# Attention top-32 selection: seven blocks of 82 to 84 columns, masks of three tiles on ScalarE, and a check that reads a PSUM bank

## The chip, the cores and the metric

The kernel runs on one core of one Trainium2 chip. A core has a matrix engine (TensorE, in the profile PE, its weight loads PEld), a vector engine (VectorE, DVE), an activation engine (ScalarE, ACT), a general engine (GpSimd, POOL), SyncE (SP), which issues most transfers here, and 16 DMA engines. They run side by side, each through its own list of instructions in order, and wait for each other by semaphores. Work memory is SBUF; TensorE writes to PSUM, eight banks that VectorE and ScalarE can read and write too. The metric is the time of one execution on the device in microseconds (us), the median of three.

## The reference

Three layers run one after the other on float32 data. Attention has 4 batches, 8 heads, 576 positions of width 64; the two layers of experts that follow are not touched by the change.

```python
B, H, S, D = q.shape                                   # 4, 8, 576, 64
scores = scale * np.matmul(q, k.transpose(0, 1, 3, 2))
kth = np.partition(scores, -32, axis=-1)[..., -32:-31]  # the 32nd largest of a row
scores = np.where(scores >= kth, scores, -1e9)
scores = scores - np.max(scores, axis=-1, keepdims=True)
attn = np.exp(scores)
attn = attn / (np.sum(attn, axis=-1, keepdims=True) + 1e-09)
return np.matmul(attn, v)
...
x = _moe_ref(x, ...)      # router over 8 experts, one expert per token, 512 -> 1024 -> 512
return _moe2_ref(x, ...)  # 512 -> 2048 -> 512 for every token
```

So each of 18,432 rows of 576 scores needs its exact 32nd largest value; everything below it is dropped.

## The kernel before

**Tiles.** Two heads make a pair, and a pair's 1152 rows make nine tiles of 128 rows (j = 0 to 7 hold four tiles of one head each, j = 8 the last 64 rows of both heads). 16 pairs make 144 tiles.

**One tile.** TensorE computes its scores into PSUM (L165), ScalarE copies them to SBUF (`ss`, L176). VectorE takes the eight largest of each of eight blocks of 72 columns (L186, one MAX8 a block), which gives 64 candidates (`cand`). From these it takes the largest 24 in five instructions: the largest eight (L195), these struck out (L196), the next eight (L197), struck out (L198), the next eight (L199); the 24th goes into `w`. ScalarE compares the whole row with the 24th candidate (L252: `sg`, with the count in `c1`) and takes the exponential (L257). GpSimd multiplies row and signs (L263, `z`), so that all that lies above the 24th turns negative, and VectorE takes the largest eight of z (L208): with the count, these and the 24th hold the 32nd value, which L209 picks out (`kth`). The mask row >= kth is made by VectorE (L218) for most tiles, and for the tiles of a pair named in `SIGN`, j = 0 and j = 4, by ScalarE as a sign (L243), for which VectorE first makes a negative threshold of one column (L214, `nk`). GpSimd multiplies mask and exponential (L269, `pm`), TensorE transposes the product in five pieces (L289), ScalarE copies these to SBUF (L294, L296) and drops the sign's negative values on the way, and TensorE multiplies them with the values (L310).

**What sets the order.** The loop in `tiles` runs over iterations. In iteration i each step works on another tile, by the lags in `ORDER` (L351): scores and their copy for tile i+1, block maxima for i, selection, signs and z for i-1, the exponential for i-2, the 32nd value for i-3, the mask for i-4, transposes for i-6, output for i-7. In VectorE's list of an iteration (`dve_step`) the mask comes first, then block maxima and selection steps take turns, then the steps of the 32nd value. In ScalarE's list the sign mask comes before the copies of the transposes, and these before the copy of the next scores, the sign and the exponential. Small work of other kinds is put into the gaps: transposing the next pair's queries and keys (L145, L151, in the iterations of j = 1, 3, 5), dividing the outputs (L342 to L346), turning a finished pair for the router (L573 to L584), and for each finished batch the router's products and steps (L593 to L703) and its scatter (L728).

**The check.** For each batch `check` looks whether any 32nd or 24th value is not positive, and notes it in `bad`; then a general path runs at the end in place of the fast one. Its steps stand one an iteration behind the router's steps of the batch. `own` hands out columns of one PSUM bank that VectorE uses for small operands.

**After attention** come the expert products on TensorE (from about 530 us), whose first weights and rows are loaded while attention ends.

Of the kernel before, what the change touches and what calls it, by code (L numbers as in the profile page):

```python
# [12 lines left out]
F32 = mybir.dt.float32  # L13
# [4 lines left out]
OP = mybir.AluOpType  # L18
AX = mybir.AxisListType
PSUM = bass.MemoryType.PSUM  # L20

P = 128
B, H, S, D = 4, 8, 576, 64
NPAIR = H // 2
KB = 8
BW = S // KB
CK = 116
NCK = 5
# [6 lines left out]
def thirds(a):  # L35
    return a.rearrange("p (a b) -> p a b", a=3)


class Job:


    def __init__(self, n, b, hp, j, st):
        self.n, self.b, self.hp, self.j, self.st = n, b, hp, j, st
        self.pre = None
# [5 lines left out]
class Attention:  # L50
    def __init__(self, ctx, tc, q, k, v, sb, ident):
        self.tc, self.nc = tc, tc.nc
        self.q, self.k, self.v = q, k, v
        self.ident = ident
        nc = self.nc
        self.wk = ctx.enter_context(tc.tile_pool(name="attn", bufs=2))
        self.ps = ctx.enter_context(tc.tile_pool(name="attn_ps", bufs=1, space=PSUM))
        one = ctx.enter_context(tc.tile_pool(name="attn_one", bufs=1))

        self.new_pt1()  # L60
        self.new_po()
        self.new_s()

        self.bank = self.ps.tile([P, 512], F32, name="own")
        self.taken = 0
        self.vt = []
        for i in range(3):
            t = one.tile([CK, NCK, 2, D + 1], F32, name=f"vt{i}")
            nc.gpsimd.memset(t, 0.0)
            nc.gpsimd.memset(t[:, :, :, D:D + 1], 1.0)  # L70
            self.vt.append(t)
        self.qm = []
        for i in range(2):
            t = one.tile([P, P], F32, name=f"qm{i}")
            nc.gpsimd.memset(t, 0.0)
            self.qm.append(t)
        self.pb = []
        for i in range(3):
            t = one.tile([P, NCK * CK], F32, name=f"pm{i}")
            nc.vector.memset(t[:, S:], 0.0)  # L80
            self.pb.append(t)
        vsel = one.tile([P, 9, 2], F32, name="vsel")
        nc.gpsimd.iota(vsel, pattern=[[2, 9], [1, 2]], base=S - 2 * TOP, channel_multiplier=0,
                       allow_small_or_imprecise_dtypes=True)
        nc.vector.memset(vsel[:, 0, 1:2], -float(S + 1))
        self.vsel = self.own(18).rearrange("p (a b) -> p a b", b=2)
        nc.vector.tensor_copy(self.vsel, vsel)
        self.rden = self.own(6)
        self.fac = self.own(2)
        nc.vector.memset(self.fac[:, 0:1], -0.125)  # L90
        nc.vector.memset(self.fac[:, 1:2], TINY)
        self.bad = sb.tile([P, 1], F32, name="bad")
        nc.vector.memset(self.bad, 0.0)
        self.per = NPAIR * 9
# [11 lines left out]

    def check(self, st):

        wk, n, v = self.wk, self.per, self.nc.vector
        kth, sm = st  # L110
        d = wk.tile([P, n], F32, name="ckd", bufs=1)
        m = wk.tile([P, 1], F32, name="ckm", bufs=1)
        return [NEXT, lambda: v.tensor_tensor(d, kth, sm[:, :, 1], op=OP.min),
                NEXT, lambda: v.tensor_reduce(m, d, axis=AX.X, op=OP.min),
                NEXT, lambda: v.scalar_tensor_tensor(self.bad, m, 0.0, self.bad, op0=OP.is_le, op1=OP.max)]

    def load(self, b, hp):
        nc = self.nc
# [59 lines left out]
    def dve_step(self, A, Bt, C, M, E, slot):  # L178


        nc, wk = self.nc, self.wk
        blocks, sel, fin = [], [], []
        if A is not None:
            A.cand = wk.tile([P, KB, 8], F32, name="cand", bufs=3)
            for i in range(KB):
                blocks.append(lambda i=i: nc.vector.max(A.cand[:, i], A.ss[:, i * BW:(i + 1) * BW]))  # L186
        if Bt is not None:
            cf = Bt.cand.rearrange("p a b -> p (a b)")
            m = Bt.n % self.per
            if m % 2 == 0:  # L190
                self.w = wk.tile([P, 2, 32], F32, name="w", bufs=3)
            ww = self.w
            w = Bt.w = ww[:, m % 2]
            Bt.sm = Bt.bt[1][:, m]
            sel = [lambda: nc.vector.max(w[:, 0:8], cf),  # L195
                   lambda: nc.vector.match_replace(cf, w[:, 0:8], cf, -1e30),  # L196
                   lambda: nc.vector.max(w[:, 8:16], cf),  # L197
                   lambda: nc.vector.match_replace(cf, w[:, 8:16], cf, -1e30),  # L198
                   lambda: nc.vector.max(w[:, 16:24], cf)]  # L199
            if m % 2:  # L200
                sel.append(lambda: nc.vector.tensor_tensor(
                    Bt.bt[1][:, m - 1:m + 1], ww[:, :, 0:24:23], self.fac[:, None, :].to_broadcast([P, 2, 2]),
                    op=OP.mult))
        if C is not None:
            i = C.n % self.per
            C.kth = C.bt[0][:, i:i + 1]
            scr = wk.tile([P, 9, 2], F32, name="scr", bufs=4)
            fin = [lambda: nc.vector.max(C.w[:, 24:32], C.z),  # L208
                   lambda: nc.vector.scalar_tensor_tensor(scr, self.vsel, C.c1,  # L209
                                                          C.w[:, 23:32, None].to_broadcast([P, 9, 2]), op0=OP.is_equal,  # L210
                                                          op1=OP.mult, accum_out=C.kth)]
            if C.j in self.SIGN:
                C.nk = wk.tile([P, 1], F32, name="nk", bufs=2)
                fin.append(lambda: nc.vector.tensor_scalar(C.nk, C.kth, -TINY, None, op0=OP.mult))  # L214
        fin_at = 5
        chain = sel[:5]
        if M is not None and M.j not in self.SIGN:
            nc.vector.tensor_scalar(self.new_mask(M), thirds(M.ss), M.kth, None, op0=OP.is_ge)  # L218
        for i in range(KB):
            if blocks:  # L220
                blocks[i]()
            if chain:
                chain.pop(0)()
            elif sel[5:]:
                sel.pop()()
                sel = sel[:5]
            if i >= fin_at - 1 and fin:
                fin.pop(0)()
            if i == 2 and E is not None and self.dve_evac(E):
                self.st_evac_v(E)  # L230
            slot(i)
        for f in fin:
            f()

    SIGN = (0, 4)

    def new_mask(self, T):
        T.mg = self.wk.tile([P, 3, S // 3 + 4], F32, name="mg")[:, :, :S // 3]
# [2 lines left out]
    def st_sign2(self, T):  # L241
        if T.j in self.SIGN:
            self.nc.scalar.activation(self.new_mask(T), thirds(T.ss), AF.Sign, bias=T.nk)  # L243
# [191 lines left out]
NEXT = None  # L435
# [1172 lines left out]
```

## Time and profile before

| | |
|---|---|
| median of 3 runs (lowest, highest) | 1232.92 us (1229.69, 1234.66) |
| profiled execution, its own time | 1234.27 us |
| span of its instructions | 1232.6 us |
| TensorE busy, of the span | 1175.5 us |
| VectorE busy | 895.8 us |
| GpSimd busy | 721.5 us |
| ScalarE busy | 688.5 us |

The profile is one execution; its own time is 1.67 us longer than the span of its instructions, and it lies 1.35 us above the median of the runs. The busy times are means over stages with different limits, so they have to be read stage by stage: the attention stage fills about the first 510 us. An instruction's duration in the profile overlaps with the next one on the same engine; how much an engine's list gets longer by it is read from the starts of two that follow each other, or from its share of a chain of waits that runs on this engine alone.

### The profile page before, as it was taken

To read this page: it belongs to the slowest core of one execution; us is meant where nothing else is said; L and a number is where in the kernel's file an instruction comes from. 1 tells how busy PE (TensorE), PEld (TensorE's weight loads), DVE (VectorE), ACT (ScalarE), POOL (GpSimd) and SP (SyncE) were. 2 spreads that over 40 slices of the span, in tenths; PEclk is the share of its full clock that TensorE was granted. 3 is DMA by queue.
4 is the path that set the end of the run, shared out by engine and by line. 5 is a ranking of instruction groups with operands and counts; after the bars stand their busy time and mean duration, and the time that the engine had idled before them with its cause. 6 is when DMAs were issued, how large, how long until landed. Compare 5 with 4: busy or idle time off the path is not lost.

```text
span 1232.6 us, 23943 instructions
## 1 busy us (share of the span) xinstructions
PE 1175.5 (95%) x7729; PEld 1028.1 (83%) x7729; DVE 895.8 (73%) x3769; ACT 688.5 (56%) x1479; POOL 721.5 (59%) x684
## 2 busy tenths in 40 slices
PE   7999999999998999998999899989999999999996
PEld 4777778777876787898999799989899898898995
DVE  5999999999999999885635376767657564454450
ACT  5899989988898988744434255523222322122120
POOL 4898888998899888852424344445335342333331
PEclk9999999999999999888999999989999999999998
DMA  5343221311131113158866678452232121222211
GB/s 132 105 109 103 57 55 52 93 52 49 53 90 36 33 32 121 39 139 194 221 148 202 169 216 222 145 138 86 69 103 86 52 69 54 84 69 69 78 43 55
DMA packets 121539, 120.86 MB, mean 98 GB/s; under 512 B 73380, under 2 KB 91300, under 8 KB 121404
## 3 DMA queue, kind: packets, MB, share of 16 engines
q1 hardware_dynamic: 118492, 109.78, 32.6%
q0 software_dynamic: 2912, 9.46, 2.1%
q8 instruction: 63, 1.03, 0.4%
q14 instruction: 72, 0.59, 0.2%
HBM read 84.25 MB, written 33.92 MB: 96 GB/s over the span
## 4 chain that ended last, share of the span: by engine, by line
PE 46%; DVE 40%; DMA 7%; issue 2%; ACT 2%; POOL 2%; POOLq 0%; SPq 0%; DVEq 0%; ACTq 0%
DVE cand L186 12%; PE mm L990 9%; PE mm L991 9%; PE mm L989 9%; DVE w L208 7%; DVE mg L218 6%; PE mm L1207 5%; PE mm L1206 5%; PE mm L1205 5%; DMA yt<-y 5%; DVE cand L198 2%; DVE cand L196 2%; DMA raw<-in_moe_w 2%; DVE scr L209 2%; DVE w L195 1%
## 5 line engine op out<-in xcount | busy, mean ns | idle before, releaser
L989 PE MATMUL mm<-xT,wt 128*128 128x256 f32 (+7 forms) x852 | 249.4, 293 | 12.0 <-ACT y L1125 6.1
L990 PE MATMUL mm<-xT,wt 128*128 128x256 f32 (+7 forms) x852 | 250.1, 294 | 4.4 <-DVE xT L984 4.3
L186 DVE MAX8 cand<-ss 128x8 f32<-128x72 f32 x1152 | 244.9, 222 | 10.1 <-ACT ss L176 10.1
L991 PE MATMUL mm<-xT,wt 128*128 128x256 f32 (+7 forms) x852 | 249.5, 293 | 0.0
L263 POOL TENSOR_TENSOR z<-ss,sg 128x576 f32<-128x576 f32 x143 | 201.7, 1411 | 64.3 <-ACT sg L252 45.0
L310 PEld LDWEIGHTS po<-vt,pT 116*128 116x128 f32 x1440 | 175.1, 192 | 36.6 <-issue 23.9
L269 POOL TENSOR_TENSOR pm<-e,mg 128x576 f32<-128x576 f32 x141 | 198.8, 1410 | 0.5
L310 PE MATMUL po<-vt,pT 116*128 116x130 f32 x1440 | 197.3, 283 | 1.8 <-ACT pc L342 1.7
L1190 POOL TENSOR_TENSOR hT<-xr,hT 128x256 fp32r<-128x256 f32 x144 | 106.3, 743 | 153.2 <-ACT hT L1189 146.2
L989 PEld LDWEIGHTS mm<-xT,wt 128*128 128x128 f32 x852 | 164.3, 193 | 13.8 <-ACT y L1125 6.6
L1189 ACT ACTIVATE hT<-xr 128x256 fp32r<-128x256 f32 x144 | 59.0, 416 | 200.8 <-DVE xr L1186 194.3
L165 PE MATMUL s<-qk 64*128 64x288 f32 x512 | 166.3, 447 | 3.8 <-ACT ss L176 3.2
L990 PEld LDWEIGHTS mm<-xT,wt 128*128 128x128 f32 x852 | 164.5, 193 | 5.5 <-DVE xT L984 4.5
L991 PEld LDWEIGHTS mm<-xT,wt 128*128 128x128 f32 x852 | 164.9, 194 | 0.0
L924 POOL TENSOR_TENSOR wt<-raw,wt 128x1024 fp32r<-128x1024 f32 x29 | 76.7, 2648 | 98.0 <-ACT wt L923 97.8
L1185 DVE TENSOR_SCALAR xr<-mm,alpha 128x256 f32<-128x256 f32 x144 | 69.3, 481 | 85.1 <-PE mm L991 84.3
L165 PEld LDWEIGHTS s<-qk 64*128 64x128 f32 x512 | 89.6, 194 | 43.2 <-issue 13.4
L252 ACT ACTIVATE sg<-ss,w 128x576 f32<-128x576 f32 x144 | 111.5, 775 | 19.4 <-DVE w L199 17.6
L289 PE MATMUL pt<-ident,pm 128*116 128x128 f32 x720 | 107.3, 278 | 12.5 <-DVE tT L584 7.4
L176 ACT ACTIVATE ss<-s 128x576 f32<-128x576 f32 x144 | 94.0, 653 | 36.6 <-PE s L165 36.3
L257 ACT ACTIVATE e<-ss,sm 128x576 f32<-128x576 f32 x144 | 110.7, 769 | 0.0
L208 DVE MAX8 w<-z 128x8 f32<-128x576 f32 x144 | 106.9, 743 | 0.8 <-POOL z L263 0.8
(248 smaller groups left out, 2490.7 us busy)
## 6 DMA issues: line engine op xcount, KB each, us to landing
raw<-in_moe_w SPq DMA_DIRECT2D x60, 512.0 KB
xr<-yt SPq DMA_DIRECT2D x18, 512.0 KB
xs<-zeros SPq DMA_DIRECT2D x8, 1028.0 KB
raw<-in_moe_w_in SPq DMA_DIRECT2D x16, 512.0 KB
raw<-in_moe_w_out SPq DMA_DIRECT2D x16, 512.0 KB
yt<-zeros SPq DMA_DIRECT2D x8, 704.0 KB
rows<-in_q SPq DMA_DIRECT2D x32, 144.0 KB
rows<-in_k SPq DMA_DIRECT2D x32, 144.0 KB
```

The costliest lines, as they stand in the source:

```text
L165: nc.tensor.matmul(s[:, g, :HALF], qs, t["qk"][hs, S + g * HALF:S + (g + 1) * HALF], start=True, stop=True)
L186: blocks.append(lambda i=i: nc.vector.max(A.cand[:, i], A.ss[:, i * BW:(i + 1) * BW]))
L208: fin = [lambda: nc.vector.max(C.w[:, 24:32], C.z), lambda: nc.vector.scalar_tensor_tensor(scr, self.vsel, C.c1, C.w[:, 23:32, None].to_br ...
L252: nc.scalar.activation(T.sg, T.ss, AF.Sign, bias=T.w[:, 23:24], scale=-ABOVE, accum_out=T.c1)
L257: nc.scalar.activation(T.e, T.ss, AF.Exp, bias=T.sm[:, 0:1], scale=0.125)
L263: eng.tensor_tensor(T.z, T.ss, T.sg, op=OP.mult)
L269: eng.tensor_tensor(thirds(T.pm[:, :S]), thirds(T.e), T.mg, op=OP.mult)
L289: nc.tensor.transpose(o, T.pm[:, c * CK:(c + 1) * CK], self.ident)
L310: nc.tensor.matmul(po[:, i:i + 2, :], T.pT[:, c], rhs, start=(c == 0), stop=(c == NCK - 1))
L989: nc.tensor.matmul(ps, wh, xh, start=first, stop=False)
L990: nc.tensor.matmul(ps, wh, xl, start=False, stop=False)
L991: nc.tensor.matmul(ps, wl, xh, start=False, stop=last)
```

## The change

Three edits. `KB` goes from 8 to 7: seven blocks, six of 82 columns and the last of 84, so 56 candidates in place of 64; the loop in `dve_step` still has eight places, the eighth without a block. `SIGN` goes from tiles 0 and 4 to tiles 0, 3 and 6 of each pair. `check` makes three reductions (of `kth`, of every second column of `sm`, of the two results) into three columns of VectorE's PSUM bank, and its last step reads the result there; before it took the minimum of the two SBUF tensors, reduced it to SBUF and read it there. One step more, so one iteration more.

```diff
-KB = 8
+KB = 7
 BW = S // KB
...
+        self.least = self.own(3)
...
-        d = wk.tile([P, n], F32, name="ckd", bufs=1)
-        m = wk.tile([P, 1], F32, name="ckm", bufs=1)
-        return [NEXT, lambda: v.tensor_tensor(d, kth, sm[:, :, 1], op=OP.min),
-                NEXT, lambda: v.tensor_reduce(m, d, axis=AX.X, op=OP.min),
-                NEXT, lambda: v.scalar_tensor_tensor(self.bad, m, 0.0, self.bad, op0=OP.is_le, op1=OP.max)]
+        return [NEXT, lambda: v.tensor_reduce(m[:, 0:1], kth, axis=AX.X, op=OP.min),
+                NEXT, lambda: v.tensor_reduce(m[:, 1:2], sm[:, :, 1], axis=AX.X, op=OP.min),
+                NEXT, lambda: v.tensor_reduce(m[:, 2:3], m[:, 0:2], axis=AX.X, op=OP.min),
+                NEXT, lambda: v.scalar_tensor_tensor(self.bad, m[:, 2:3], 0.0, self.bad, op0=OP.is_le, op1=OP.max)]
...
-                blocks.append(lambda i=i: nc.vector.max(A.cand[:, i], A.ss[:, i * BW:(i + 1) * BW]))
+                blocks.append(lambda i=i: nc.vector.max(A.cand[:, i], A.ss[:, i * BW:(i + 1) * BW if i + 1 < KB else S]))
...
-        for i in range(KB):
-            if blocks:
+        for i in range(8):
+            if i < len(blocks):
                 blocks[i]()
...
-    SIGN = (0, 4)
+    SIGN = (0, 3, 6)
```

On VectorE, from the 32nd value of the third pair's tile 6 on (`w` from `z`, then `scr`), the list before goes on to that tile's mask; line numbers are the same in both kernels here, and the last row strikes out candidates:

```order
L208 MAX w<-z 128x8
L186 MAX cand<-ss 128x8
L209 SCALAR_TENSOR_TENSOR scr,kth<-own,c_1480,w 128x18
L186 MAX cand<-ss 128x8 x2
L218 TENSOR_SCALAR mg<-ss,kth 128x3x192
L186 MAX cand<-ss 128x8
L195 MAX w<-cand 128x8
L186 MAX cand<-ss 128x8
L196 MATCH_REPLACE cand<-w,cand 128x64
```

and now, at the same place:

```order
L208 MAX w<-z 128x8
L186 MAX cand<-ss 128x8
L209 SCALAR_TENSOR_TENSOR scr,kth<-own,c_1458,w 128x18
L186 MAX cand<-ss 128x8
L214 TENSOR_SCALAR nk<-kth 128x1
L186 MAX cand<-ss 128x8
L195 MAX w<-cand 128x8
L186 MAX cand<-ss 128x8
L196 MATCH_REPLACE cand<-w,cand 128x56
```

The eighth block maximum and the mask are gone from the row, a product of one column stands in their place, and the candidates are 56.

On ScalarE, one iteration of the third pair (j = 1, with a copy `qk` of the next pair's transposed queries and keys), before:

```order
L257 ACTIVATE e<-ss,sm 128x576
L294 ACTIVATE pT<-pt_1112 116x512
L296 ACTIVATE pT<-pt_1113 116x128
L176 ACTIVATE ss<-s 128x576
L151 ACTIVATE qk<-pt_1133 128x384
L252 ACTIVATE sg,c_1161<-ss,w 128x576
```

and now:

```order
L257 ACTIVATE e<-ss,sm 128x576
L243 ACTIVATE mg<-ss,nk 128x3x192
L294 ACTIVATE pT<-pt_1097 116x512
L296 ACTIVATE pT<-pt_1098 116x128
L176 ACTIVATE ss<-s 128x576
L151 ACTIVATE qk<-pt_1120 128x384
L252 ACTIVATE sg,c_1145<-ss,w 128x576
```

The mask of tile 6 of the pair before has come in ahead of the copies of the transposes and of the scores. The lists of TensorE, GpSimd and SP hold the same rows in the same order in both kernels.

## Rows read from the trace of the kernel before

**Rows 1.** The page's 40 slices, busy tenths of TensorE and VectorE.
```profile
PE   7999999999998999998999899989999999999996
...
DVE  5999999999999999885635376767657564454450
```

**Rows 2.** Stretches: length, busy of PE, PEld, DVE, ACT, POOL, clock, DMA share, GB/s.
```profile
135.50:165.40 29.90, 29.01 (x191) 22.66 (x189) 29.90 (x181) 27.98 (x63) 26.58 (x23) 1.00 0.22 58
165.40:198.10 32.70, 31.97 (x225) 26.24 (x223) 32.31 (x204) 27.55 (x61) 26.48 (x24) 1.00 0.20 53
...
482.40:508.70 26.30, 22.66 (x149) 18.01 (x149) 25.69 (x153) 22.96 (x49) 25.55 (x25) 1.00 0.44 156
```

**Rows 3.** Chain of waits inside the plain pair (135.5 to 165.4 us), share by line.
```profile
by line: DVE cand L186 33.0%; DVE w L208 19.9%; DVE mg L218 16.7%; DVE cand L196 5.9%; DVE cand L198 5.9%; DVE scr L209 4.5%; DVE w L195 3.8%; DVE w L199 3.8%; DVE w L197 3.8%; DVE tT L584 0.9%; DVE sm L201 0.8%; DVE r L344 0.6%; DVE own L3
```

**Rows 4.** Waits in the same pair: waiter, releaser, us in total, times, longest.
```profile
ACT sg L252 <- DVE w L199: 1.1, 4, 0.3
...
PEld pt L289 <- DVE tT L584: 1.0, 1, 1.0
...
PEld po L310 <- ACT pc L342: 0.9, 2, 0.5
ACT ss L176 <- PE s L165: 0.8, 2, 0.6
```

**Rows 5.** Timeline of VectorE at a one-column product: start, us, instruction.
```profile
156.95 0.14 DVE L214 TENSOR_SCALAR nk<-kth 128x1 f32<-128x1 f32 x1
157.00 0.23 DVE L186 MAX8 cand<-ss 128x8 f32<-128x72 f32 x1
```

**Rows 6.** Timeline of ScalarE, one iteration with a mask.
```profile
157.48 0.76 ACT L243 ACTIVATE mg<-ss,nk 128x576 f32<-128x576 f32 x1
158.14 0.57 ACT L294 ACTIVATE pT<-pt 116x512 f32<-116x512 f32 x1
...
158.78 0.64 ACT L176 ACTIVATE ss<-s 128x576 f32<-128x576 f32 x1
159.31 0.77 ACT L252 ACTIVATE sg<-ss,w 128x576 f32<-128x576 f32 x1
...
160.06 0.77 ACT L257 ACTIVATE e<-ss,sm 128x576 f32<-128x576 f32 x1
160.73 0.59 ACT L294 ACTIVATE pT<-pt 116x512 f32<-116x512 f32 x1
```

**Rows 7.** Timeline of VectorE at the checks of the first two batches, one of the third.
```profile
247.55 0.53 DVE L113 TENSOR_TENSOR ckd<-kth,sm 128x36 f32<-128x36 f32 x1
248.01 0.80 DVE L218 TENSOR_SCALAR mg<-ss,kth 128x576 f32<-128x576 f32 x1
...
254.43 1.62 DVE L115 SCALAR_TENSOR_TENSOR bad<-ckm,bad 128x1 f32<-128x1 f32 x1
255.97 0.80 DVE L218 TENSOR_SCALAR mg<-ss,kth 128x576 f32<-128x576 f32 x1
...
380.14 2.19 DVE L115 SCALAR_TENSOR_TENSOR bad<-ckm,bad 128x1 f32<-128x1 f32 x1
382.25 0.80 DVE L218 TENSOR_SCALAR mg<-ss,kth 128x576 f32<-128x576 f32 x1
...
508.23 0.17 DVE L114 TENSOR_REDUCE ckm<-ckd 128x1 f32<-128x36 f32 x1
508.32 0.80 DVE L218 TENSOR_SCALAR mg<-ss,kth 128x576 f32<-128x576 f32 x1
```

**Rows 8.** Timeline of GpSimd beside the second of these places.
```profile
254.63 1.40 POOL L269 TENSOR_TENSOR pm<-e,mg 128x576 f32<-128x576 f32 x1
255.99 0.61 POOL L346 TENSOR_TENSOR xb<-pc,r 128x256 f32<-128x256 f32 x1
```

**Rows 9.** Stretches around the first fall of TensorE's clock (columns of rows 2).
```profile
505.00:510.00 5.00, 4.23 (x33) 4.04 (x33) 4.90 (x29) 3.92 (x9) 4.82 (x6) 0.87 0.22 43
510.00:515.00 5.00, 5.00 (x26) 4.83 (x26) 4.11 (x13) 2.84 (x7) 4.85 (x6) 0.50 0.25 79
```

More of the change, by code (lines that the diff above doesn't have):

```diff
@@ L107, in check @@
     def check(self, st):
-        wk, n, v = self.wk, self.per, self.nc.vector
+        v, m = self.nc.vector, self.least
         kth, sm = st
-        d = wk.tile([P, n], F32, name="ckd", bufs=1)
-        m = wk.tile([P, 1], F32, name="ckm", bufs=1)
-        return [NEXT, lambda: v.tensor_tensor(d, kth, sm[:, :, 1], op=OP.min),
-                NEXT, lambda: v.tensor_reduce(m, d, axis=AX.X, op=OP.min),
-                NEXT, lambda: v.scalar_tensor_tensor(self.bad, m, 0.0, self.bad, op0=OP.is_le, op1=OP.max)]
+        return [NEXT, lambda: v.tensor_reduce(m[:, 0:1], kth, axis=AX.X, op=OP.min),
+                NEXT, lambda: v.tensor_reduce(m[:, 1:2], sm[:, :, 1], axis=AX.X, op=OP.min),
+                NEXT, lambda: v.tensor_reduce(m[:, 2:3], m[:, 0:2], axis=AX.X, op=OP.min),
+                NEXT, lambda: v.scalar_tensor_tensor(self.bad, m[:, 2:3], 0.0, self.bad, op0=OP.is_le, op1=OP.max)]
     def load(self, b, hp):
```

## The prediction

> **What bounds the kernel now.** I read the page's forty slices first. The first 16 slices (to about 500 us) are the attention stage, and there VectorE stands at 9 in nearly every slice; after it VectorE falls to 3 to 7 while TensorE stays at 9, so everything that the diff touches lies in the first stage [rows 1]. Next the busy time of each engine in stretches of one pair of heads (nine tiles). A plain pair (135.5 to 165.4) takes 29.9 us: VectorE is busy in 29.90 of them, TensorE in 29.01, ScalarE in 27.98, GpSimd in 26.58; a pair in which the router's products run (165.4 to 198.1) takes 32.70 us, with TensorE at 31.97 and VectorE at 32.31 [rows 2]. Then the chain of waits inside one plain pair: it is VectorE alone, line after line, so its shares are start-to-start times of VectorE's instructions [rows 3]. Last the waits in the same pair, to see how far the others are behind it: ScalarE waits 1.1 us for VectorE's 24th candidate and 0.8 us for the scores, which with its 27.98 busy makes up the 29.9; TensorE's weight loads wait 1.0 us for VectorE's late copy and 0.9 us for ScalarE's copy of the output [rows 4]. So VectorE sets the pace, and ScalarE and TensorE would follow it down by only 1 to 2 us a pair. That is the point of the case: a large cut on the bound engine with the next two close behind.
>
> **The change part by part.** The lists of TensorE, GpSimd and SP hold the same instructions in the same order, so no transfer moves; only VectorE and ScalarE differ.
>
> Block maxima. In the plain pair L186 has 33.0% of 29.9 us in 72 instructions, 0.137 us each at 72 columns; the scan of z (L208) has 19.9% in nine, 0.661 us at 576 columns; L199 has 3.8% in nine, 0.126 us at 64 columns [rows 3]. The slope between 64 and 576 columns is 0.535 us over 512, 1.045 ns a column. At 82 columns that gives 0.1475 us and at 84 0.1495, so seven cost 1.034 us where eight cost 1.096: 0.062 us a tile. No row shows 82 columns: if width cost nothing the saving would be 0.137, and by the steeper step from 64 to 72 columns (0.011 us for 8) it would be 0.04; I take the slope, which spans the width. Five instructions of the selection read 56 columns in place of 64: 5 x 8 x 1.045 ns = 0.042 us (0 to 0.055). Together 0.104 us a tile (0.04 to 0.19), and 15.0 us over 144 tiles.
>
> Masks. L218 has 16.7% of the pair in seven instructions, 0.713 us each [rows 3]. Each moved mask leaves one small product on VectorE (L214), 0.05 us from its start to the next instruction's [rows 5]. Sixteen pairs move one each: 16 x 0.66 = 10.6 us off VectorE. On ScalarE each adds what the present one takes from its start to the next, 0.66 us (157.48 to 158.14) [rows 6]; sixteen are 10.6 us there. In ScalarE's queue the mask stands ahead of the evacuation of the transposes (0.64 us) and of the copy of the next scores (0.53 us), and VectorE, TensorE's output products and GpSimd wait for these three [rows 6].
>
> The check. VectorE stood 0.46 us in the minimum of two SBUF tensors (247.55 to 248.01), and 1.54 and 2.11 us in the last step, whose operands are 128 x 1 and both in SBUF; the reduction between takes 0.09 [rows 7]. That last step ended at 255.97, and GpSimd's product that had begun at 254.63 gave way to the next at 255.99: VectorE stood still for GpSimd [rows 8]. The new version has three reductions and one step, each with at most one SBUF tensor. At 0.09 for a reduction and 0.15 for the nearest step of that kind with a PSUM operand (L209, 4.5% in nine) a check costs 0.42 us [rows 3, 7]. So the two checks inside the stage save (0.46 + 0.09 + 1.54 - 0.42) + (0.46 + 0.09 + 2.11 - 0.42) = 3.9 us. If each of the two reductions that read SBUF stood still for one GpSimd product of 1.4 us, four such stalls would turn that into a loss of 1.7. The other two checks come after 500 us, beside TensorE's tail, and count as nothing; without that cover they would give 2 us each.
>
> Sum on VectorE: 15.0 + 10.6 + 3.9 = 29.5 us. Not all of it lies on the path. At the start (to 46 us) TensorE and ScalarE feed the first tiles, and in the last stretch (482.4 to 508.7) TensorE's 22.66 us and VectorE's 25.69 us of 26.3 show both waiting for GpSimd; of the 3.3 us that fall to these tiles I take 0.8 [rows 2]. Between lie 14 pairs with 9 x 0.104 + 0.66 = 1.6 us each.
>
> What is late next? In a plain pair ScalarE has 27.98 + 0.66 = 28.64 us of work, so the pair can shrink by 1.26 us before ScalarE is never idle; TensorE's waits of rows 4 allow some 1.9. ScalarE's wait for the 24th candidate is a wait for the engine that gets faster, so it goes; its wait for the scores partly stays, since scores still follow the transposes on TensorE. The ends are therefore +1.26 us gained (no wait left) and -0.64 (both waits kept, mask on top). I take 1.1, near the upper end: the larger wait is for VectorE itself, and of the smaller one I let 0.16 us stay. In pairs with the router's products TensorE idles for 0.7 us by its busy row; I take 0.9 for three such pairs, and 1.0 for the three with the router's long steps. Sum: six plain pairs 6.6, three 2.7, three 3.0, the two pairs with a check 2.2 + 3.9, the edges 0.8: 19.2 us.
>
> The profiled execution took 1234.27 us (span 1232.6 and 1.7 around it), the median of the runs is 1232.92; the same 19 us off each give 1215 and **1214 us**, and I predict the median.
>
> **Rivals.**
> *VectorE keeps the lead.* All pairs give their 1.6 us: 14 x 1.6 + 3.9 + 1.5 = 27.8, so 1205 us. For it: VectorE has no idle time, and the others' waits shrink when it is faster. Against it: ScalarE's 28.64 us of work against VectorE's new 28.3 in a plain pair.
> The Trainium skill (Perfetto Trace Analysis, Identifying the Most-Contended Engine) has TensorE's headroom read from the busy time of its weight loads and not of its matmuls; that row says 22.66 of 29.9 us, so by this rule TensorE is a quarter idle, does not bind, and this rival's 1205 follows. The waits in the trace agree with it only in part: the weight loads wait for other engines for 1.9 us in the two rows shown, not for 7.
>
> *ScalarE sets the pace.* It keeps its 0.8 us for the scores: 28.64 + 0.8 = 29.44, 0.46 us gained a pair; 14 x 0.46 + 3.9 = 10.3, so 1223 us. For it: the mask of tile 6 falls in the iteration that also copies transposed keys, next to one with two more copies. Against it: ScalarE stands ready and waiting for VectorE four times in this pair, so most of its queue has slack.
>
> *Slower: the mask is simply added.* Place: ScalarE's queue ahead of L294 and L176. If both its waits stay (1.9 us, because they come from the order on TensorE and VectorE and not from pace), a pair takes 28.64 + 1.9 = 30.54, 0.64 us more; over 16 pairs 10.2, less 3.9 for the checks, is +6.3, so 1239 us. It decides as soon as less than 0.4 us a pair of these waits goes. Against it: the larger of the two waits names VectorE's L199, which comes earlier.
>
> *Not what it says:* with seven blocks of eight maxima a row whose large scores crowd into one block loses some, and too many lost ones would run the general path after the fast one, a loss far outside the range. The 24 wanted are 3.4 a block on average, and the eight maxima of z make up for up to eight lost, so I leave this below 1 in 100.
>
> **How the numbers follow.** Forecast 0.48, VectorE keeps the lead 0.15, ScalarE sets the pace 0.22, mask added 0.15. The range of 1204 to 1228 reaches from the first rival past the second, and leaves out the last and a little below; its width also holds the bounds of block maxima (0.04 to 0.19 us a tile, 6 to 27 us). About 0.5%, 6 us, is what a measurement of this kernel tells from no change. The forecast and the first rival are faster (0.63), of the second three quarters (0.16); the rest of it and half of the last, where some of the waits go, are the same (0.13); the other half is slower (0.08).
>
> **What would show it.** In the changed profile a plain pair of some 28.8 us; L186 in 63 instructions of about 0.148 us on the chain and selections of about 0.118; ScalarE's wait for L199 near nothing, and for the first time a few waits of VectorE's L186 for ScalarE's copy of the scores; the check's last step at 0.15 to 0.2 us; the end of attention about 19 us earlier and the rest of the same length. The forecast fails if the pair stays above 29.4 us (ScalarE holds it), or if TensorE's granted clock, which now reads 0.87 of full speed from 505 to 510 us and 0.50 (the lower of its two levels) from 510 to 515 [rows 9], falls inside the attention stage too: 10 us at the lower level are 5 us lost.

## The result and the profile after

| | before | after |
|---|---|---|
| median of 6 runs each, alternating on one chip (lowest, highest) | 1232.57 us (1227.69, 1235.4) | 1218.05 us (1215.8, 1221.36) |
| profiled execution, its span | 1234.27, 1232.6 us | 1218.64, 1216.8 us |
| VectorE, TensorE busy | 895.8, 1175.5 us | 871.8, 1171.7 us |

The ratio is 0.9891, with a 95% interval of 0.9869 to 0.9913: 13.4 us faster (10.7 to 16.1), where 18.9 were forecast. Faster, in the range, and 4 us short of the forecast time. The steps behind it came out less evenly, and one of them by an effect that the prediction had put down only as a danger.

The slices of the page that answer to [rows 1]:

```profile
PE   7999999999999999998999899989999999999996
...
DVE  5999999999999999776545376666657564454440
```

VectorE still shows 9 in the same slices; only in the two slices where attention ends it is 7 for 8. A 9 says "90% or more" and not "this is the bound". The stretches (columns of [rows 2]) say more: a plain pair, a pair with the router's products, a pair with a check and a scatter, and the end of attention.

```profile
131.90:160.40 28.50, 28.49 (x190) 22.61 (x188) 28.50 (x173) 28.20 (x64) 26.76 (x23) 1.00 0.24 60
160.40:192.90 32.50, 32.50 (x234) 27.17 (x233) 30.76 (x194) 28.32 (x63) 27.76 (x25) 1.00 0.20 53
223.60:254.30 30.70, 28.68 (x187) 22.66 (x188) 29.04 (x177) 28.74 (x64) 29.98 (x30) 1.00 0.30 86
469.30:496.40 27.10, 23.52 (x157) 18.72 (x156) 25.09 (x145) 23.66 (x52) 26.37 (x26) 1.00 0.44 152
```

A plain pair went from 29.9 to 28.5 us, and TensorE has no idle time left in it (28.49 busy); VectorE has none either (28.50), so the two are level and only the experiments below tell them apart. The router pair hardly moved (32.6 to 32.5, by the table below), and now VectorE idles there (30.76 busy). In the third row GpSimd is the busiest, 29.98 of 30.70. The chain of waits inside the same three pairs, share by line:

```profile
by line: PE po L310 39.0%; PE s L165 36.1%; PE pt L289 17.3%; PE pt L145 5.3%; PE pt L573 3.0%; PE pt L577 0.4%; issue 0.0%
...
by line: PE po L310 34.2%; PE s L165 30.1%; PE pt L289 15.2%; PE pt L593 11.4%; PE pt L145 4.6%; PE pt L597 3.5%; PE pt L573 1.8%; PE pt L577 0.3%
...
by line: POOL pm L269 22.3%; DVE cand L186 12.4%; issue 11.5%; DVE mg L218 9.9%; DVE w L208 6.4%; POOL xs L728 6.2%; POOL z L263 4.4%; PE po L310 3.7%; ACT pT L294 2.9%; DVE cand L196 2.4%; POOL xb L346 2.0%; DVE w L195 1.9%; DVE cand L198 
```

In the plain pair the chain was VectorE alone [rows 3]; now it is TensorE alone. In the third pair GpSimd's products (L269, 22.3%) lead the chain, and its scatter (L728, 6.2%) stands in it. The waits in the plain pair (none of them is VectorE's: the waits of L186 for ScalarE's copy of the scores, which the prediction expected, did not come here):

```profile
PEld po L310 <- issue: 1.5, 4, 0.4
POOL z L263 <- ACT sg L252: 1.0, 3, 0.5
...
ACT ss L176 <- PE s L165: 0.2, 1, 0.2
```

Both waits of ScalarE that [rows 4] show are gone or nearly gone (1.1 us for L199, 0.8 to 0.2 for the scores). In the third pair (223.6 to 254.3) others stand:

```profile
PEld pt L289 <- POOL pm L269: 2.0, 2, 1.0
DVE mg L218 <- POOL pm L269: 1.7, 3, 1.1
```

TensorE's transposes and VectorE's masks both wait for GpSimd. The check in that pair, on VectorE's timeline, answers to [rows 7]:

```profile
242.68 0.19 DVE L112 TENSOR_REDUCE own<-kth 128x1 f32<-128x36 f32 x1
...
245.42 0.18 DVE L113 TENSOR_REDUCE own<-sm 128x1 f32<-128x36 f32 x1
...
249.45 0.15 DVE L114 TENSOR_REDUCE own<-own 128x1 f32<-128x2 f32 x1
...
252.91 0.15 DVE L115 SCALAR_TENSOR_TENSOR bad<-own,bad 128x1 f32<-128x1 f32 x1
```

No step of it stands still any more: 0.15 us where 1.62 and 2.19 stood. The two reductions that read SBUF took 0.19 and 0.18, so the bound of a loss (four new stalls) is out.

The table adds up the time from one L199 to that of the next pair (nine tiles, from a pair's first L199, the end of a tile's selection, to the next pair's first; pairs counted from 0), in the two profiled executions:

| | before | after | gain | forecast |
|---|---|---|---|---|
| six plain pairs: 1 to 4, 8, 12 | 179.22 | 171.57 | 7.65 | 6.6 |
| three with router products: 5, 9, 13 | 97.86 | 97.61 | 0.25 | 2.7 |
| three with the router's long steps: 6, 10, 14 | 94.90 | 93.15 | 1.75 | 3.0 |
| two with check and scatter: 7, 11 | 64.48 | 61.19 | 3.29 | 6.1 |
| edges (up to the end of pair 0, pair 15) | 73.74 | 74.21 | -0.47 | 0.8 |
| **attention up to the last L199** | 510.20 | 497.73 | 12.47 | 19.2 |
| the rest of the span | 722.4 | 719.1 | 3.3 | 0 |

The last line can't be put down to the change: apart from the last two checks the code after attention is the same, and in the fourteen profiled executions of this document the rest goes from 715.7 to 722.7 us. A part of such differences is TensorE's clock: one stretch in which it is granted at half lasted 6.8 us at 706.6 before and 3.4 us at 694.4 after. Over 51 runs of before, the time at the lower level, worked out as twice (1 - mean clock) times the span, goes from 27 to 55 us (43 on the mean; 37 in the six runs after), and within a kernel a run is some 0.3 us longer for each us of it. At that price the 3.4 us are 1 of the 3.3.

### The profile page after: what moved, and what is told of

Read it like the earlier page. It is cut to its first block, busy times and chain, and to the rows that moved or that the text cites. A ratio compares the mean times of both kernels' runs of the same rounds, so it can differ in the third digit from the quotient of the medians.

```text
span 1216.8 us, 23815 instructions
## 1 busy us (share of the span) xinstructions
PE 1171.7 (96%) x7729; PEld 1028.1 (84%) x7729; DVE 871.8 (72%) x3629; ACT 695.0 (57%) x1495; POOL 725.6 (60%) x684
## 3 DMA queue, kind: packets, MB, share of 16 engines
q1 hardware_dynamic: 118492, 109.78, 32.5%
## 4 chain that ended last, share of the span: by engine, by line
PE 72%; DVE 12%; DMA 5%; ACT 3%; POOL 3%; issue 3%; SPq 1%; POOLq 0%; ACTq 0%; DVEq 0%
PE mm L990 10%; PE mm L991 10%; PE mm L989 10%; PE po L310 9%; PE s L165 8%; PE mm L1207 6%; PE mm L1206 6%; PE mm L1205 6%; PE pt L289 4%; DMA yt<-y 4%; DVE cand L186 3%; DVE mg L218 2%; DVE w L208 2%; POOL pm L269 2%; PE pt L145 1%
## 5 line engine op out<-in xcount | busy, mean ns | idle before, releaser
L186 DVE MAX8 cand<-ss 128x8 f32<-128x82 f32 (+1 forms) x1008 | 231.7, 232 | 14.2 <-ACT ss L176 14.2
L263 POOL TENSOR_TENSOR z<-ss,sg 128x576 f32<-128x576 f32 x143 | 204.9, 1433 | 47.8 <-ACT sg L252 27.4
L269 POOL TENSOR_TENSOR pm<-e,mg 128x576 f32<-128x576 f32 x141 | 199.1, 1412 | 2.7 <-ACT mg L243 2.2
L176 ACT ACTIVATE ss<-s 128x576 f32<-128x576 f32 x144 | 94.9, 659 | 30.2 <-PE s L165 29.4
```

The source lines that it names most:

```text
L263: eng.tensor_tensor(T.z, T.ss, T.sg, op=OP.mult)
L269: eng.tensor_tensor(thirds(T.pm[:, :S]), thirds(T.e), T.mg, op=OP.mult)
```

## The experiments

Four theories stand in the expectations. **T**: TensorE has become the bound, at about 28.5 us a plain pair, and had long been it in the router pairs. **V**: VectorE still sets the pace. **A**: ScalarE does. **C**: VectorE's stop at the old check makes TensorE idle so long that its clock falls inside attention. All eight combinations of the three edits were run, which gives the table below; "pairs with check" are pairs 7, 8, 11 and 12 together, since a delay in 7 or 11 runs into the next. The runs of before that stood beside the others have medians from 1228.74 to 1234.93 us, so ratios are compared, and not times.

| blocks | masks | check | ratio (95%) | pairs 1 to 4 | router pairs | pairs with check | last L199 |
|---|---|---|---|---|---|---|---|
| 8 | 2 | old | 1 | 119.5 | 97.9 | 124.2 | 510.2 |
| **7** | 2 | old | 0.9958 (0.9942, 0.9974) | 117.3 | 97.6 | 125.7 | 508.2 |
| 8 | **3** | old | 1.0016 (0.9986, 1.0047) | 116.9 | 98.3 | 123.9 | 508.4 |
| 8 | 2 | **new** | 0.9957 (0.9938, 0.9977) | 119.5 | 97.9 | 120.3 | 507.0 |
| **7** | **3** | old | 0.9973 (0.9956, 0.9990) | 114.5 | 97.6 | 126.3 | 507.0 |
| **7** | 2 | **new** | 0.9920 (0.9892, 0.9948) | 117.2 | 97.6 | 118.8 | 502.0 |
| 8 | **3** | **new** | 0.9921 (0.9898, 0.9945) | 116.9 | 98.3 | 119.0 | 500.7 |
| **7** | **3** | **new** | 0.9891 (0.9869, 0.9913) | 114.5 | 97.6 | 118.2 | 497.7 |

**Block maxima alone** (1230.00 us beside 1234.92).

```diff
-KB = 8
+KB = 7
```

> Before with seven blocks alone; masks and check as before. Theory T (TensorE becomes the pace-setter at 28.5 us a plain pair, and already is in the pairs with the router's products): a plain pair goes from 29.9 to about 29.0, since VectorE's new time stands above TensorE's 28.5, but the pairs with router products lose under 0.3 us; in all some 9 us off, about 1223.5. Rival V (VectorE remains the pace-setter everywhere): 14 pairs by 0.93 us, 13 us off, about 1219.5, router pairs shorter by 0.9.

The plain pair came out at 29.2 to 29.3 us, VectorE busy throughout; T and V had both put it at 29.0. The router pairs decide between them: they lost 0.08 us each, where V had 0.9. But the kernel missed both times, and a part of that is what follows at the first check. Stretches:

```profile
133.50:162.80 29.30, 28.64 (x191) 22.75 (x191) 29.30 (x173) 27.88 (x63) 26.79 (x23) 1.00 0.23 59
255.00:260.00 5.00, 3.15 (x24) 2.48 (x23) 5.00 (x29) 3.68 (x8) 5.00 (x4) 0.98 0.03 7
260.00:265.00 5.00, 5.00 (x18) 3.57 (x17) 5.00 (x28) 4.03 (x11) 2.94 (x4) 0.50 0.00 0
```

TensorE idles for 1.85 us and then has its lower level, 0.50 of full speed (1.2 GHz), which the kernel before shows nowhere inside attention.

**Masks alone** (1235.50 us).

```diff
-    SIGN = (0, 4)
+    SIGN = (0, 3, 6)
```

> Before with masks of tiles 0, 3 and 6 on ScalarE alone. T: plain pair 29.9 - 0.66 = 29.2, router pairs under 0.3 us shorter, about 7 us off in all, 1225.5. V: 14 x 0.66 = 9.3 off, 1223. Rival A (ScalarE sets the pace): no gain or a loss, 1232 to 1239, with ScalarE at full length of the pair.

```profile
133.50:162.80 29.30, 28.59 (x189) 22.67 (x188) 29.30 (x182) 28.31 (x64) 26.70 (x23) 1.00 0.23 59
```

The plain pair went from 29.88 to 29.23 us, just the 0.66 of the prediction, with ScalarE at 28.31: nothing is "simply added". Still the kernel as a whole gained nothing. In this execution the four pairs with check gave 0.3 us in place of four times 0.66, with the lower clock for 3.4 us from 384.6; the router pairs got 0.14 us longer each, and the first and last pair 1.7 together. The ten runs had 51 us at the lower level on the mean, where the runs of before beside them have 45.

**The new check alone** (1229.94 us).

```diff
-        return [NEXT, lambda: v.tensor_tensor(d, kth, sm[:, :, 1], op=OP.min),
...
+        return [NEXT, lambda: v.tensor_reduce(m[:, 0:1], kth, axis=AX.X, op=OP.min),
...
```

> Before with the new check alone. V: the two pairs with a check lose 1.7 and 2.2 us, 3.9 in all, 1228.7. T with GpSimd as the limit of these two pairs (it has the scatters there): 1.0 to 1.5 us each at most, 1229.5 to 1230.5. In both the last step of the check takes 0.15 to 0.2 us. If T holds, the gains of the three single edits add up to at least 5 us more than the 14.5 of all three; if V holds, to the same.

A plain pair, and the pair with the first check (32.06 before):

```profile
135.50:165.40 29.90, 29.01 (x189) 22.65 (x190) 29.90 (x181) 27.98 (x64) 26.60 (x23) 1.00 0.22 58
229.80:260.10 30.30, 28.75 (x188) 22.48 (x187) 30.30 (x187) 28.33 (x63) 29.59 (x29) 1.00 0.30 87
```

Pairs 7 and 11 gave 1.79 and 2.15 us, together the 3.9 that the prediction worked out, and not T's 1.0 to 1.5 each; the other pairs between the edges moved by 0.02 us at most. The three edits alone sum to about 8.5 us by their ratios (5.2 - 2.0 + 5.3), together they gave 13.4. T had expected the opposite, singles that sum to more. The intervals of the four ratios together leave nearly 6 us open, so the ratios alone would not show it; the traces below have to.

**The old check in the changed kernel** (1229.08 us) tests theory C.

```diff
-        return [NEXT, lambda: v.tensor_reduce(m[:, 0:1], kth, axis=AX.X, op=OP.min),
...
+        return [NEXT, lambda: v.tensor_tensor(d, kth, sm[:, :, 1], op=OP.min),
...
```

> The changed kernel with the check of before (seven blocks, three masks). Stall alone: the two pairs with a check get back 1.7 and 2.2 us, 1222. Theory C (the stall of VectorE lets TensorE idle, and in the faster kernel that lets its clock fall): besides the stall a half-clock stretch of 3 to 7 us at the end of one or both of these pairs, the next pair longer by 1 to 2 us, 1224 to 1230, with a wider spread from run to run than the changed kernel.

Four engines at that place, one after the other. VectorE (start, us, instruction):

```profile
250.07 2.50 DVE L115 SCALAR_TENSOR_TENSOR bad<-ckm,bad 128x1 f32<-128x1 f32 x1
252.49 0.80 DVE L218 TENSOR_SCALAR mg<-ss,kth 128x576 f32<-128x576 f32 x1
```

GpSimd beside it:

```profile
250.58 1.40 POOL L269 TENSOR_TENSOR pm<-e,mg 128x576 f32<-128x576 f32 x1
251.94 0.61 POOL L346 TENSOR_TENSOR xb<-pc,r 128x256 f32<-128x256 f32 x1
252.52 0.65 POOL L346 TENSOR_TENSOR mx<-pc,r 64x64 f32<-64x64 f32 x2
```

ScalarE (in brackets its idle time before, and the releaser):

```profile
254.84 0.78 ACT L252 ACTIVATE sg<-ss,w 128x576 f32<-128x576 f32 x1 [2.65 <-DVE w L199]
...
257.00 0.58 ACT L294 ACTIVATE pT<-pt 116x512 f32<-116x512 f32 x1
```

TensorE, with its idle time:

```profile
257.62 0.55 PE L145 MATMUL pt<-ident,rows 96*128 96x96 f32 x4 [2.50 <-ACT pT L294]
```

And stretches of 5 us (columns of [rows 2]):

```profile
250.00:255.00 5.00, 5.00 (x31) 3.55 (x28) 5.00 (x16) 2.12 (x6) 4.85 (x7) 1.00 0.04 9
255.00:260.00 5.00, 2.50 (x17) 2.38 (x16) 5.00 (x32) 5.00 (x11) 4.25 (x4) 0.84 0.01 2
260.00:265.00 5.00, 5.00 (x28) 3.85 (x27) 4.37 (x29) 3.95 (x10) 3.05 (x3) 0.82 0.00 0
```

One step of one column holds VectorE for 2.50 us, until GpSimd begins the third of the products shown; the sign waits 2.65 us for the late candidate; in ScalarE's queue the copy of the transposes stands behind the sign, so TensorE idles 2.50 us; and soon after it has work again its clock falls to the lower level, for 3.4 us (0.84 and 0.82 in the last two rows). The pair takes 33.09 us and the next 30.14, where the new check has 30.69 and 28.51. The spread of the runs (5.0 us) is not wider than that of the changed kernel (5.6), though C had expected so. The old check is thus what brings the lower clock into attention, as C says. How long TensorE idles does not decide it alone. Seven of the eight places with the old check in the four kernels that take work from VectorE have a fall of the clock behind them, after 1.69 to 2.51 us of idle TensorE; the eighth, the first check with masks alone, has 2.46 us of idle time and none. The kernel before idles there for 1.23 and 1.78 us without a fall. Masks alone at its first check (the first two rows), and before at its second:

```profile
255.00:260.00 5.00, 2.54 (x16) 1.64 (x15) 5.00 (x34) 2.97 (x7) 4.85 (x5) 1.00 0.03 7
260.00:265.00 5.00, 5.00 (x39) 4.24 (x37) 5.00 (x28) 5.00 (x13) 3.71 (x3) 1.00 0.00 0
...
385.00:390.00 5.00, 3.30 (x24) 2.75 (x24) 5.00 (x29) 4.73 (x12) 4.51 (x4) 1.00 0.02 3
```

What else it takes stays open. The sum of the pairs with check gives the price: the new check is worth 3.9 us there alone, 6.9 with seven blocks, 4.9 with three masks, 8.1 with both. Of the 4.1 us between the first and the last of these, the two stops themselves give 1.2 (2.50 and 2.51 us for 1.62 and 2.19); the rest is left for what the idle time and the lower clock cost further on. The masks alone show the two apart: against the same masks with the new check, the first stop (2.27 us, no fall) costs its two pairs 2.25 us, the second and shorter one (1.69 us, with a fall) 2.68. The pairs with check hold 3.2 us of the 5.4 by which the edits together shorten attention by more than the three singles do; 2.2 lie in the first and last pair, which differ by up to 3.2 us between the fourteen executions. In all four kernels that take work from VectorE and keep the old check (blocks alone, masks alone, this one, and the last of this section) the clock falls soon after the first or the second check; in none with the new check does it fall before 494 us.

**Each of the other edits taken back** (1226.30 us without the masks, 1224.28 without the blocks).

```diff
-    SIGN = (0, 3, 6)
+    SIGN = (0, 4)
```

> The changed kernel with the masks of two tiles, j = 0 and 4, on ScalarE as before; seven blocks and the new check stay. T (TensorE sets the pace of a plain pair at 28.5 us, and a stop of VectorE at the old check is what lets its clock fall): VectorE paces the plain pairs again at 29.2 us, as with seven blocks alone, router pairs stay at 32.5, no stretch at the lower clock inside attention since the check is the new one; six plain pairs lose 0.7 each: 1222 to 1223 us. Additive rival (the single edits add up; masks alone were worth +0.6 us the wrong way): 1218 us or a little less. If the clock falls inside attention all the same, so that the check is not the cause: 1226 us or more.

```diff
-KB = 7
+KB = 8
```

> The changed kernel with eight blocks of 72 columns as before; three masks on ScalarE and the new check stay. T: as the last one, plain pairs at 29.2 us with VectorE never idle, router pairs at 32.5, no lower clock inside attention: 1222 to 1223 us. Additive rival (blocks alone were worth 4.9 us): 1223 us as well, but then the kernel without the masks must come out at 1218. If the clock falls inside attention: 1226 us or more.

By profile both came out as T has it: plain pairs of 29.2 us, router pairs as expected (32.54 and 32.76), no lower clock inside attention, the last L199 4.3 and 3.0 us later than after. T's time is 0.991 to 0.992 of the 1232.57 us of before; the ratios, 0.9920 and 0.9921, agree, with four runs each. The additive rival's 1218, 0.988 of it, lies outside the first one's interval (0.9892, 0.9948), if narrowly. By the ratios the masks are worth 3.6 to 4.4 us with the new check and -1.8 to -2.0 with the old, each to within 3 to 4 us.

**More work for TensorE**, after (1230.34 us, ratio 0.9981) and before (1235.11 us, ratio 1.0011 (0.9986, 1.0035)): the first of the five transposes of a tile is done twice, some 0.11 us a tile, 1.0 a pair.

```diff
-        for c in range(NCK):
+        for c in (0,) + tuple(range(NCK)):
```

> The changed kernel with TensorE's first transpose of each tile done twice into the same place (about 0.11 us more of TensorE a tile, 1.0 us a pair, the result the same). T (TensorE is the pace-setter after the change): a plain pair goes from 28.52 to 29.5 us and a pair with router products from 32.54 to 33.5; about 13 us more in all, 1231. V (VectorE is still the pace-setter): plain pair within 0.2 us, 1218 to 1221.

> The same doubled transpose in the kernel before. T: plain pair stays within 0.2 us of 29.89, since TensorE has 1.4 us to spare there, but the pairs with router products, which T takes for TensorE-bound already, go from 32.62 to about 33.5; some 4 us more, 1237. Rival (TensorE not the limit in the router pairs): those stay within 0.2 us too, time as before.

Plain pair and router pair, in the changed kernel with the extra transpose:

```profile
133.70:163.00 29.30, 29.30 (x199) 23.75 (x197) 28.78 (x172) 28.31 (x64) 26.85 (x23) 1.00 0.23 58
163.00:196.40 33.40, 33.40 (x244) 28.15 (x243) 31.02 (x194) 28.20 (x63) 27.57 (x25) 1.00 0.19 52
```

and in the kernel before with it:

```profile
136.90:166.80 29.90, 29.48 (x199) 23.71 (x199) 29.90 (x182) 27.94 (x63) 26.58 (x23) 1.00 0.22 57
166.80:199.90 33.10, 32.74 (x235) 27.32 (x233) 32.28 (x203) 27.72 (x61) 26.23 (x23) 1.00 0.19 52
```

After the change the same work costs 0.8 us in either kind of pair shown (0.5 to 0.8 over the six plain ones; T had 1.0), and the last L199 comes 8.4 us later. Before it, it costs nothing in a plain pair and 0.55 in a router pair (33.17 from 32.62). So TensorE bounds the plain pairs now and did not before; in router pairs it was nearly the bound already: 0.55 of the 0.8 us shows there, though its busy row had 0.7 us of idle time, and the lighter lists of VectorE in the table (blocks, masks or both) shorten three router pairs by 0.3 us at most. The chain of waits did not tell this. In that pair of the kernel before it runs mostly through VectorE:

```profile
by line: DVE cand L186 24.8%; DVE w L208 14.1%; DVE mg L218 13.4%; POOL z L263 4.3%; DVE cand L198 4.2%; POOL pm L269 4.2%; DVE cand L196 4.2%; issue 3.8%; DVE scr L209 3.2%; DVE w L195 3.1%; DVE w L199 2.7%; DVE w L197 2.7%; ACT sg L252 2.
```

**Less work for VectorE**: six blocks of 96 columns (1221.88 us), and four masks on ScalarE (1218.74 us, two runs), both on the changed kernel.

```diff
-KB = 7
+KB = 6
```

> The changed kernel with six blocks of 96 columns and 48 candidates: VectorE loses another 0.06 + 0.042 us a tile, 0.9 us a pair, and nothing else changes. T: plain pair still 28.5 us, VectorE idle for about 0.9 of it, time within 3 us of the changed kernel's 1218. V: plain pair 27.6, about 13 us off, 1205.

```profile
132.50:161.20 28.70, 28.49 (x190) 22.67 (x188) 28.06 (x163) 28.23 (x64) 26.56 (x23) 1.00 0.23 60
```

```diff
-    SIGN = (0, 3, 6)
+    SIGN = (0, 2, 4, 6)
```

> The changed kernel with masks of tiles 0, 2, 4 and 6 on ScalarE: 0.66 us a pair less on VectorE, 0.66 more on ScalarE. V: plain pair 27.9, about 9 us off, 1209. T: nothing gained, 28.5. T with ScalarE close behind (28.2 us busy of 28.5 in the changed profile): ScalarE becomes the pace-setter at 28.9 or a little more, 3 to 8 us slower than the changed kernel, 1221 to 1226.

```profile
130.90:159.70 28.80, 28.77 (x190) 22.69 (x189) 28.13 (x173) 28.75 (x65) 26.84 (x23) 1.00 0.23 60
```

V falls: VectorE now idles some 0.65 us a pair in both and nothing is gained (0.9895 and 0.9890 against before; plain pairs up to 0.2 us longer). With six blocks the chain still names VectorE in the plain pair:

```profile
by line: DVE cand L186 26.0%; DVE mg L218 16.9%; DVE w L208 16.1%; DVE cand L198 5.0%; DVE cand L196 5.0%; POOL z L263 4.9%; DVE scr L209 3.9%; DVE w L199 3.1%; issue 3.1%; DVE w L197 3.1%; DVE w L195 3.1%; ACT sg L252 3.0%; ACT mg L243 2.1
```

With engines as level as here, the chain does not say which one a cut would pay on. The second run also bounds A: with another mask ScalarE is busy 28.75 of 28.80, level with TensorE, so it has no more to give; with three masks it had 0.3 us to spare. The 1221 to 1226 us that the expectation put for ScalarE close behind did not come.

**A third mask buffer** (1218.11 us, ratio 0.9870 (0.9845, 0.9895)) asks what holds pairs 7 and 11; one buffer of the scores is given up for it.

```diff
-        T.ss = wk.tile([P, S], F32, name="ss", bufs=7)
+        T.ss = wk.tile([P, S], F32, name="ss", bufs=6)
...
-        T.mg = self.wk.tile([P, 3, S // 3 + 4], F32, name="mg")[:, :, :S // 3]
+        T.mg = self.wk.tile([P, 3, S // 3 + 4], F32, name="mg", bufs=3)[:, :, :S // 3]
```

> The changed kernel with three buffers for the mask in place of two (and six for the scores in place of seven, to make room). It tells what holds the pairs with a scatter (7 and 11 of 0 to 15, 30.7 and 30.5 us now), where VectorE's masks wait 1.7 us for GpSimd's products. G (GpSimd's own work sets their pace, 29.98 of 30.70 us busy): these pairs stay at 30.3 us or more, 1217.5 to 1218.5 us. M (the two mask buffers hold them): they fall to 29 us, 1215 us. Plain pairs stay at 28.5 by both.

Pair 7 and the pair behind it:

```profile
222.90:252.80 29.90, 27.85 (x183) 22.14 (x184) 29.18 (x177) 28.00 (x63) 29.18 (x29) 1.00 0.30 87
252.80:281.90 29.10, 29.10 (x193) 23.08 (x192) 28.46 (x173) 28.82 (x65) 28.62 (x24) 1.00 0.24 61
```

Neither theory has it in full. Pair 7 fell to 29.91, below what G allowed, but pair 8 rose from 28.51 to 29.08: the two together took 58.99 where they took 59.20. VectorE's masks no longer wait, TensorE's transposes still wait 2.0 us for GpSimd's product, and in pair 8 TensorE, never idle, works off what was put off in pair 7. The buffers set where the delay shows. That GpSimd sets its size is read from these waits and from its busy time; no run makes GpSimd's work in these pairs lighter, so it is not shown.

**Where the empty place stands** (1223.44 us beside 1228.74, ratio 0.9962 (0.9940, 0.9984)): seven blocks alone, with the place that has no block at the start of an iteration (the edit is shown against the run with blocks alone).

```diff
-            if i < len(blocks):
-                blocks[i]()
+            if 8 - i <= len(blocks):
+                blocks[i - 8]()
```

> The kernel before with seven blocks alone, but the place without a block is the first of the eight in an iteration and not the last, so that two block maxima stand between the step that picks the 32nd value and the mask that reads it, where one is left in the changed kernel. If the block term came out at 0.072 us a tile in place of 0.104 because that mask now waits for its threshold (0.045 us, in the seven tiles of a pair whose mask VectorE makes), a plain pair falls from 29.25 us with seven blocks alone to 28.95, VectorE still never idle, and the block maximum ahead of the mask starts 0.145 to 0.15 us before it, not 0.19. If the missing 0.03 us is the price of the wider blocks themselves, it stays at 29.25.

VectorE with the empty place last (blocks alone), from the step that makes the threshold to the mask:

```profile
144.15 0.22 DVE L209 SCALAR_TENSOR_TENSOR scr<-own,c,w 128x18 f32<-128x18 f32 x1
...
144.30 0.24 DVE L186 MAX8 cand<-ss 128x8 f32<-128x84 f32 x1
144.49 0.81 DVE L218 TENSOR_SCALAR mg<-ss,kth 128x576 f32<-128x576 f32 x1
```

and with the empty place first, at an iteration's end without a mask and at one with:

```profile
141.91 0.23 DVE L186 MAX8 cand<-ss 128x8 f32<-128x84 f32 x1
142.18 0.22 DVE L195 MAX8 w<-cand 128x8 f32<-128x56 f32 x1
...
144.51 0.39 DVE L186 MAX8 cand<-ss 128x8 f32<-128x82 f32 x2
144.82 0.80 DVE L218 TENSOR_SCALAR mg<-ss,kth 128x576 f32<-128x576 f32 x1
```

From the last block to the mask it is 0.19 us (144.30 to 144.49) with one block between, and 0.148 on the mean of seven with two: that wait went as expected. The pair did not get shorter (29.20, 28.95 expected). In the two tiles of a pair whose mask ScalarE makes, the selection (L195) now comes right behind the last block of the candidates it reads and starts 0.27 us after it, where 0.153 was usual; in all nine its own next neighbour starts 0.129 after it in place of 0.118, and a block right behind a block 0.158 after it. The gap moved to other neighbours in the list. The missing 0.03 us a tile is thus not the width of the blocks: what follows a block of 82 columns starts 0.145 us after it (ahead of L196) where it was 0.135 with 72, the 0.010 worked out.

## Why the prediction came out as it did

**Right: what bounds the kernel, and the plain pairs.** VectorE was the bound. A plain pair gave 1.28 us on the mean of six (1.36 in pairs 2, 3, 4, 8 and 12), where 1.1 was taken. The masks gave 0.66 as worked out, the check's two stops 3.9 when removed alone.

**Wrong engine behind it, and a limit that hardly took hold.** "What is late next" was ScalarE, with 28.64 us of work. It was TensorE, at 28.5. The two limits lie 0.14 us apart, so the time of a plain pair came out nearly right by luck. Nor was 28.64 a floor for ScalarE: it is busy 28.20 us in the changed pair, which is shorter than that. And the forecast had 1.6 us cut from VectorE, of which the next engine lets 1.1 through; the runs have 0.65 from blocks alone and 0.65 from masks alone, and the pair gave about their sum. VectorE and TensorE are level at 28.5 in the changed pair, and TensorE binds only what is cut beyond that. The waits of rows 4 were read as "some 1.9" us of slack a pair for TensorE; the pair shrank by 1.4.

The Trainium skill (Perfetto Trace Analysis, Identifying the Most-Contended Engine) reads TensorE's headroom from the share of its peak that it reaches and from the busy share of its weight loads. These are busy 22.61 of 28.50 us in the very pair whose chain is TensorE alone, and adding to TensorE lengthens the pair by 0.8 us. Here the weight loads mislead, and the rival built on them (1205 us) fell.

**The step that failed most: router pairs.** "In pairs with the router's products TensorE idles for 0.7 us by its busy row; I take 0.9 for three such pairs", the prediction says. They gave 0.08 each. Most of the idle time in the row was not headroom, as the extra transpose in the kernel before shows: with it a router pair grew by 0.55 us of the 0.8 that the same work costs where TensorE is never idle. This and the pairs with the long steps (1.8, 3.0 forecast) make 3.7 of the 6.7 us that attention fell short.

**Pairs with a check.** "2.2 + 3.9" assumed that what VectorE sheds by blocks and masks adds to the check's 3.9. It did not: 3.3 in place of 6.1 (6.0 in place of 8.3 with the pairs behind them). With the check alone these pairs took 30.27 us, and with blocks and masks as well 30.69 and 30.50. GpSimd with its scatter (29.98 of 30.70 us busy) looks like the next limit there, by its busy time and the waits for it; that is argued and not shown. The prediction named GpSimd for the last stretch only.

**The block term** was mis-sized: 0.104 us a tile forecast, 0.072 found with blocks alone (0.65 in the plain pairs 3, 4 and 12). The slope over columns and the shorter selections were right. What was left out is that the eighth block also stood between the threshold and the mask that reads it; putting the gap elsewhere brought the wait from 0.19 to 0.148 us there, and the cost came back at other neighbours.

**The danger that the prediction named** was the granted clock falling inside attention. It does, in the kernels that take the cut on VectorE and keep the old check, and the new check is what prevents it. The prediction added the check's 3.9 us to the rest as an independent term; in the presence of the other two it is worth 9.2 us up to the last L199 (507.0 to 497.7) and 10.1 by the ratios. So the forecast's total rests on the right parts, but the parts are not separable.

**The rivals.** VectorE keeps the lead: out by six blocks and by four masks. ScalarE sets the pace: out, pair 28.5 and not 29.4. Mask simply added: out by the masks alone in a plain pair; that this edit alone did not make the kernel faster has its places elsewhere: the pairs with a check, the router pairs, the first and last pair and the time at the lower clock.

Open are the 3.3 us outside attention in the profiled pair of executions, less than the 7.0 by which that rest differs among the fourteen, and how far the clock after attention depends on the edits. Also not settled is how much the masks depend on the new check: the ratios differ by some 6 us, of which the pairs with check explain 1 in the profiled executions. With eight blocks, the 6 us more at the lower level (51 against 45), at 0.3 each, explain some 2; with seven blocks the masks bring no such rise (40 against 42). No version tried beats the changed kernel by more than its measurement can tell.

## What to carry to other kernels

Before a bound engine is cut, the next limit is better found by adding work to each of the others than by their busy shares or by the chain of waits: a router pair with 0.7 us of idle time on TensorE gained next to nothing from a faster VectorE, which its chain named. Stages of one loop can have different next limits (here TensorE in plain pairs and in those with router products, and probably GpSimd with a scatter), so a gain per iteration should be multiplied only over iterations of one kind. When an edit removes a rare stop and another tightens the loop, they are worth measuring together, since the tighter loop passes the stop on to engines that had cover before.

## What the runs showed of the hardware

A VectorE step with two 128 x 1 operands in SBUF took 1.62 to 2.51 us beside GpSimd's products in attention, and 0.15 with one of the two in PSUM. In all ten places with the old check of the kernels before, blocks alone, masks alone, all but the check, and blocks with the empty place first, it begins while the same product (L263) runs on GpSimd and ends within 0.03 us of the end of a later one. In two of the ten (1.62 and 1.69 us) one more product passes it, in the others two (2.19 to 2.51 us); what decides between one and two is open. The Trainium skill (SBUF — State Buffer, SBUF: two separate sides) has a VectorE instruction with two SBUF inputs and a GpSimd one that reads SBUF exclude each other for a whole instruction; the trace agrees in kind, but the stop of 2.50 us goes through more than one of GpSimd's (1.40 and 0.61 us lie inside it), so the one that waits can be passed over again. An instruction in an in-order list is also distance: with one block maximum fewer some dependent pair of instructions comes closer, for 0.045 to 0.115 us each, wherever the empty place is put.
